# Norm broadcast and first loads in the head of a fused attention and channel-mix kernel

## The chip, the cores and the metric

One core of one Trainium2 chip runs the kernel. The metric is the device time of one execution in microseconds (us); smaller is better. The engines are named as in the profile: PE is TensorE's matmul stream and PEld its weight loads, DVE is VectorE, ACT is ScalarE, POOL is GpSimd, SP is SyncE, which here only issues DMAs.

## The reference

Two layers one after the other, in float32, for B = 4 batches of N = 6208 rows and C = 256 channels. First cross-covariance attention: the attention matrix is over channels (256 x 256), and the norms run over the rows.

```python
def _attn_ref(q, k, v, tau):
    qn = q / (np.linalg.norm(q, axis=1, keepdims=True) + 1e-06)
    kn = k / (np.linalg.norm(k, axis=1, keepdims=True) + 1e-06)
    s = kn.transpose(0, 2, 1) @ qn / tau
    s = s - s.max(-1, keepdims=True)
    a = np.exp(s)
    a /= a.sum(-1, keepdims=True) + 1e-09
    return (v @ a).astype(np.float32)
```

Then a channel mix with a shift by one row, with x the result of the first:

```python
    xk = mu_k * x + (1.0 - mu_k) * x_prev
    xr = mu_r * x + (1.0 - mu_r) * x_prev
    k = np.maximum(xk @ w_k, 0.0)
    v = k * k @ w_v
    r = 1.0 / (1.0 + np.exp(-(xr @ w_r)))
    return (r * v).astype(np.float32)
```

## The kernel before

**Tiles.** The rows of a batch are cut into NB = 12 groups of 512 and one of 64 (number 12). The second layer works on blocks of 512 rows: 48 full ones and one made of the four batches' left-over rows.

**The head.** Attention needs the whole q and k of a batch before x of that batch can be made. For batch 0 this is the head of the kernel. SP loads the rows as float32 (`head_load`, L98, eight buffers). For each piece VectorE casts to bf16 (L130 for q, L143 for k), ScalarE squares (L132, L145), and TensorE adds up norms as matmuls against a column of ones (L115) and, for k, the 256 x 256 product with q (L148, into `s_ps0`). The order is q 0 to 7, q 12, then k 0, q 8, k 1, q 9, k 2, q 10, k 3, q 11, then k 12, k 4 to k 9, and k 10 and k 11 in smaller pieces. The norms of one piece are issued after the products of the next (`flush`). Between pieces stand fillers (L194), matmuls of 512 columns into a PSUM tile that nobody reads; they keep TensorE occupied. Three of them follow k 12.

**q's norms.** All of q is in after q 11. After k 5, `root` copies the sums out of PSUM (L159) and GpSimd takes the root (L161). After k 7, `inverse` (L166, L168) adds 1e-6 and takes the reciprocal, `spread` (L176 to L179) splits the two columns into three bf16 parts, and `broadcast` (L186) makes six matmuls that spread them over all partitions into a PSUM tile of the "v" tag. After k 9 VectorE copies that tile to SBUF (`rq_bc0`, L571), where the softmax reads it (L591).

**The first loads.** GpSimd issues every load that casts from float32 to bf16, all in one queue. After k 7's cast a one-column copy (`gate`, L573) holds the queue back; then it issues v of block 0, w_k (128 x 2 x 1024 in one DMA), v of blocks 1 and 2 (L234), and q and k of the first group of batch 1 (`more_rows(1)`, L432: the group of 64 rows, which the loop's first unit reads). Behind k's root follow more groups (`more_rows`), w_r (L603), w_v (L604) and v 3. In this program a GpSimd DMA waits until the one eight before it has landed.

**From the head to the loop.** v of block 0 is transposed by TensorE (L254) and copied by ScalarE (L258); twelve fillers follow; then the softmax (L204 to L209) makes `a_sb`, and `x_first` (L275) makes the first x. It also transposes v of block 1. `wf` (L612, L613) is w_k's first 256 columns with mu folded in, for the first two up projections (L334).

**The loop.** A loop over i from -2 to 48 and j from 0 to 7 is the order of everything else, written out by hand. Step (i, j) issues the up projection of block i+1 (L339, evacuated and rectified by ScalarE at L343, squared by VectorE at L350), the gate matmul (L360) and down projection (L399, the first reader of w_v) of block i, x of block i+2 (L265, L267), the mixes (L307, L318), and units of the next batch's q and k products (L443, L447) by due times. v of blocks 2 and 3 is transposed by TensorE at j = 7 of i = -1 and i = 0; later blocks by a DMA. The first unit of batch 1 is due in step (-1, 6).

Of the kernel before, what the change touches and what calls it, by code (L numbers as in the profile page):

```python
# [14 lines left out]
OP = mybir.AluOpType  # L15
# [3 lines left out]
def kernel(  # L19
# [13 lines left out]
    nc = tc.nc  # L33
    B, N, C = q.shape
    D = C
    DF = moe_w_k.shape[1]
    P = 128
    M = 512
    S = M // P
    assert C == 256 and DF == 1024  # L40
    NB = N // M
# [47 lines left out]
    LEAD = 8  # L89
# [48 lines left out]
    def k_piece(g, s0, s1, last=False):  # L138
        rows, n = rows_of(g)
        n = s1 - s0  # L140
        f = head_load(k, 0, g, s0, s1)
        kt = pq.tile([P, S, C], BF16, name="kb", tag="kb", bufs=6)
        nc.vector.tensor_copy(kt[:rows, :n], f[:rows, :n])  # L143
        sq = pq.tile([P, S, C], BF16, name="hsq", tag="hsq", bufs=5)
        nc.scalar.activation(sq[:rows, :n], f[:rows, :n], AF.Square)  # L145
        for s in range(n):
            for ih in range(2):
                nc.tensor.matmul(s_ps0[:, ih, :], kt[:rows, s, ih * P:(ih + 1) * P], qb[g][:rows, s0 + s, :],  # L148
                                 start=first("s"), stop=last and s == n - 1, skip_group_check=True)
        flush()  # L150
        pend.append((nk_ps, "k", sq, rows, n, last))
        return kt
# [11 lines left out]
    def inverse(r, n):  # L164

        nc.vector.tensor_scalar_add(r[:, :n], r[:, :n], 1e-6)  # L166
        o = pn.tile([P, 4], F32, name="nrm_o")
        nc.vector.reciprocal(o[:, :n], r[:, :n])  # L168
        return o

    def spread(r):
        w = pn.tile([P, 3, 2], BF16, name="rw", bufs=1)
        d = pn.tile([P, 2], F32, name="rd", bufs=1)
        nc.vector.tensor_copy(w[:, 0], r[:, :2])  # L176
        nc.vector.tensor_tensor(d, r[:, :2], w[:, 0], op=OP.subtract)
        nc.vector.tensor_copy(w[:, 1], d)
        nc.vector.tensor_tensor(w[:, 2], d, w[:, 1], op=OP.subtract)  # L179
        return w  # L180

    def broadcast(w, tag, **kw):
        bc_ps = ps.tile([P, 2, P], F32, name="bc_ps", tag=tag, **kw)
        for h in range(2):
            for u in range(3):
                nc.tensor.matmul(bc_ps[:, h], w[:, u, h:h + 1].to_broadcast([P, P]), ident,  # L186
                                 start=h == 0 and u == 0, stop=u == 2, skip_group_check=True)
        return bc_ps.rearrange("p h d -> p (h d)")

    def filler(n, src=0):  # L190

        f_ps = ps.tile([P, M], F32, name="f_ps", tag="v", bufs=2)
        for u in range(n):
            nc.tensor.matmul(f_ps, ident, qb[src].rearrange("p s c -> p (s c)")[:, :M], start=u == 0, stop=u == n - 1)  # L194
# [36 lines left out]
    def v_load(i):  # L231
        b, t = blocks[i]
        v_bf = pq.tile([P, S, C], BF16, name="v_bf", tag="b2", bufs=NB + 1)
        nc.gpsimd.dma_start(v_bf, v[b, t * M:(t + 1) * M, :].rearrange("(s p) c -> p s c", p=P))  # L234
        st[i, "v"] = v_bf
# [12 lines left out]
    def v_transpose_pe(i, v_bf, s0, s1, evac):  # L248
        vT = st[i, "vT"] if (i, "vT") in st else new_vT(i)
        n = s1 - s0  # L250
        vT_ps = ps.tile([P, S, 2, P], BF16, name="vT_ps", tag="kT", bufs=3)
        for s in range(n):
            for h in range(2):
                nc.tensor.transpose(vT_ps[:, s, h], v_bf[:, s0 + s, h * P:(h + 1) * P], ident)  # L254
        if evac == "v":
            nc.vector.tensor_copy(vT[:, s0:s1], vT_ps[:, :n])
        else:
            nc.scalar.copy(vT[:, s0:s1], vT_ps[:, :n])  # L258
# [289 lines left out]
    def more_rows(n):  # L548
        while pos["load"] < min(len(loads), n):
            group_load(*loads[pos["load"]])  # L550
            pos["load"] += 1
# [6 lines left out]
    for what, g in order:  # L558
        if what == "q":
            q_piece(g, last=g == NB - 1)  # L560
        else:
            kt = k_piece(g, 0, rows_of(g)[1])
            if g < NB - LEAD or g == NB:
                filler(2 if g < NB else 3)

            if g == 5:
                nq = root(nq_ps, 2)
            if g == 7:
                bc_ps = broadcast(spread(inverse(nq, 2)), "v", bufs=2)
            if g == 9:  # L570
                nc.vector.tensor_copy(rq_bc0, bc_ps)  # L571
            if g == 7:
                nc.gpsimd.tensor_copy(gate, kt[:, 0, 0:1])  # L573
                v_load(0)
                nc.gpsimd.dma_start(w_k_sb, moe_w_k.rearrange("(ko ki) f -> ki ko f", ki=P))
                v_load(1)
                v_load(2)
                more_rows(1)
    k_piece(NB - 2, 0, 2)
    k_piece(NB - 2, 2, 4)  # L580
    k_piece(NB - 1, 0, 2)
    k_piece(NB - 1, 2, 3)
    k_piece(NB - 1, 3, 4, last=True)
    nc.sync.dma_start(mu_k_t, moe_mu_k.rearrange("(h p) -> p h", p=P))
    nc.sync.dma_start(mu_r_t, moe_mu_r.rearrange("(h p) -> p h", p=P))
    flush()
# [43 lines left out]
    for i in range(-2, NBLK):  # L630
        for j in range(8):
            T = i * 8 + j
            if i == LAST and j == 0:

                st[LAST, "res"] = pq.tile([P, S, D], F32, name="res", tag="f4", bufs=NF)
                for s in range(4):
                    gate_mm(LAST, s)
                for u in range(2):
                    gate_act(LAST, u)
            if j in (2, 6) and i != LAST:  # L640
                gate_act(i, j // 4)
            if 0 <= i + 1 < NBLK:
                up(i + 1, j)
            if j == 0 and i >= 0:
                square(i, 7)
            if j > 0 and j != 6 and 0 <= i + 1 < NBLK:
                square(i + 1, j - 1)
            if j == 5:
                finish(i, 0)
            if j == 1:  # L650
                finish(i - 1, 1)
            if i >= 0:
                if j in (0, 1, 4, 5) and i < LAST:
                    gate_mm(i, j // 4 * 2 + j % 4)
                down(i, j)
            n = i + 2
            if n == 0 and j == 0:
                x_first()
            if 0 < n < NBLK and n != LEFT:
                if j == 0:  # L660
                    x_half(n, 0)
                if j == 2:
                    x_half(n, 1)
            if n < NBLK:

                d = 4 if n != 1 else 3
                if j == d:
                    mix_delta(n)
                if j in (d + 1, d + 2):
                    mix(n, "xk", j - d - 1)  # L670
            if j == 6 and 0 <= i + 1 < NBLK:
                square(i + 1, j - 1)
            if j in (0, 1) and 0 <= i + 1 < NBLK:
                mix(i + 1, "xr", j)
            if j == 7 and 2 <= i + 3 < NPE:
                v_transpose_pe(i + 3, st.pop((i + 3, "v")), 0, S, "s")
            if j == 1 and NPE <= i + 5 < NBLK and i + 5 != LEFT:
                v_transpose_dma(i + 5)
            if j == 2 and NPE < i + 7 < NBLK and i + 7 != LEFT:
                v_load(i + 7)  # L680
            bank_x = i >= 0 and i % NB == 6 and j == 4
            if chain and (chain[0] is None or chain[0].__name__ != "bcast" or j in (4, 6)):
                f = chain.pop(0)
                if f is not None:
                    f()
                    bank_x = f.__name__ == "bcast"
            if j in (4, 6) and not bank_x or j in (3, 5) and len(norms) > 1:
                take_norm()

            near = sums and (sums[0][0] == 1 or sums[0][1] in GORD[-3:])  # L690
            if j in (2, 3, 6, 7) and near or j in (3,7) or len(sums) > (2 if near else 4):
                take_sum()
            for u in due.get(T, []):
                b, g, s = units[u]
                at = (b - 1) * (NB + 1) + GORD.index(g)
                more_rows(at + 4)
                unit(b, g, s)
                if g == GORD[-1] and s == S - 1:
                    evac_s(b)
            if i >= 0 and i // NB < B:  # L700
                bl = i // NB
                if i % NB == 2 and j == 1:
                    lst["v"] = left_load(bl)
                if i % NB == 4 and j == 3:
                    lst["t"] = left_transpose(lst["v"])
                if i % NB == 6 and j == 4:
                    left_x(bl, lst["t"])
# [35 lines left out]
```

## Time and profile before

| What | us |
|---|---|
| median of 4 runs | 507.71 (507.52 to 507.99) |
| the profiled execution | 508.19 |
| its span, first to last instruction | 506.3 |
| TensorE busy in 0 to 26 us | 17.77 |
| TensorE busy in 31 to 35 us | 3.84 of 4.00 |
| TensorE busy in 38.5 to 43 us | 4.12 of 4.50 |
| TensorE busy in 43 to 50 us | 6.76 of 7.00 |
| TensorE busy in 50 to 55 us | 4.73 of 5.00 |
| TensorE busy in 70 to 100 us | 29.79 of 30.00 |

The profile is of one execution, whose time is not the median; times of instructions are counted from the start of its span. A line of the timeline gives start, length, engine, line of the code, operation, output and inputs, shapes and how many; in brackets stands how long the engine was idle before it, and what it waited for. In a line of the chain of waits stand start, length, and who worked. A DMA's time to landing is counted from the start of its issue.

### The profile page before, as it was taken

The page shows a single profiled execution, that of the slowest core. Times are in us where ns is not written, and L with a number is a line of the kernel's source. Part 1 is how long each engine was busy: PE and PEld are TensorE (multiplying, and loading weights), DVE is VectorE, ACT ScalarE, POOL GpSimd, SP SyncE. Part 2 cuts the span into 40 slices and gives each one's busy share as a digit, 9 for nine tenths or more (in the row PEclk, how much of TensorE's full clock was granted, in tenths as well). Part 3 has the DMA queues.
Part 4 walks back from the last instruction along what each step waited for, and adds up shares of the span by engine and source line. Part 5 has one row for each costly group of instructions (what it writes and reads, how often), then busy time and mean ns, then how long its engine had stood idle before and what let it go on. Part 6 is the DMA issues. An engine that isn't in the chain of part 4 may idle for free.

```text
span 506.3 us, 9691 instructions
## 1 busy us (share of the span) xinstructions
PE 490.3 (97%) x3644; PEld 338.7 (67%) x3707; DVE 447.4 (88%) x706; ACT 430.2 (85%) x809; POOL 105.0 (21%) x145
## 2 busy tenths in 40 slices
PE   5799999999999999999999999999999999999997
PEld 2474677777676666666667666666666666666675
DVE  3468898999999999999999999999998787887875
ACT  6788999999998998998999899898787777777774
POOL 0047423332521321221441132100121000000000
PEclk9999999999999999999999999999999999999999
DMA  8999999999999999799699999963299753334123
GB/s 332 393 319 196 181 202 207 205 203 199 178 167 204 213 174 161 120 168 165 123 174 214 179 175 164 146 135 77 62 154 164 141 109 104 87 87 82 41 84 105
DMA packets 143535, 83.48 MB, mean 165 GB/s; under 512 B 51264, under 2 KB 140032, under 8 KB 143488
## 3 DMA queue, kind: packets, MB, share of 16 engines
q0 software_dynamic: 65808, 33.01, 53.1%
q1 hardware_dynamic: 77536, 49.79, 43.0%
q8 instruction: 29, 0.48, 0.4%
q14 instruction: 18, 0.15, 0.1%
q10 hardware_dynamic: 144, 0.07, 0.0%
HBM read 78.71 MB, written 25.43 MB: 206 GB/s over the span
## 4 chain that ended last, share of the span: by engine, by line
PE 83%; DVE 6%; DMA 6%; ACT 2%; issue 2%; POOL 0%; ACTq 0%; DVEq 0%
PE v_ps L399 31%; PE kT_ps L339 28%; PE g_ps L360 9%; PE xT_ps L265 7%; PE s_ps L443 6%; DMA f<-in_k_dram 3%; DMA v_bf<-in_v_dram 2%; DVE kk L350 1%; DVE acc L481 1%; DVE xk L318 1%; PE f_ps L194 1%; DVE res L412 1%; ACT kr L343 1%; DVE xr L318 1%; DMA f<-in_q_dram 1%
## 5 line engine op out<-in xcount | busy, mean ns | idle before, releaser
L343 ACT ACTIVATE kr<-kT_ps 128x512 bf16<-128x512 f32 (+1 forms) x392 | 232.3, 597 | 36.0 <-PE kT_ps L339 27.1
L399 PE MATMUL v_ps<-w_v_sb,kk 128*128 128x256 bf16 x1520 | 228.1, 273 | 0.8
L339 PE MATMUL kT_ps<-xk,w_k_sb 128*128 128x512 bf16 (+1 forms) x721 | 217.5, 377 | 1.2 <-DVE xk L318 0.3
L399 PEld LDWEIGHTS <-kk 128*128 128x128 bf16 x1520 | 148.3, 98 | 57.3
L350 DVE TENSOR_TENSOR kk<-kr 128x1024 bf16<-128x1024 bf16 (+1 forms) x196 | 133.0, 681 | 30.4 <-ACT kr L343 30.0
L447 ACT ACTIVATE sq<-qk 128x512 f32<-128x512 bf16 (+1 forms) x147 | 93.4, 635 | 0.0
L339 PEld LDWEIGHTS <-w_k_sb 128*128 128x128 bf16 x780 | 75.0, 98 | 22.4 <-issue 0.9
L360 PE MATMUL g_ps<-w_r_sb,xr 128*128 128x256 bf16 x388 | 73.6, 273 | 1.4
L267 ACT CAST X<-xT_ps 128x512 bf16<-128x512 f32 x94 | 55.5, 591 | 18.9 <-PE xT_ps L265 18.3
L318 DVE SCALAR_TENSOR_TENSOR xr<-delta,mu_r_t,X 128x512 bf16<-128x512 bf16 x96 | 71.4, 746 | 0.0
L360 PEld LDWEIGHTS <-xr 128*128 128x128 bf16 x388 | 37.9, 98 | 45.2 <-issue 1.3
L318 DVE SCALAR_TENSOR_TENSOR xk<-delta,mu_k_t,X 128x512 bf16<-128x512 bf16 x96 | 67.6, 746 | 0.0
L412 DVE SCALAR_TENSOR_TENSOR res<-res,v_ps 128x512 f32<-128x512 f32 x95 | 64.7, 681 | 0.0
L432 POOL DMA_DIRECT2D qk<-in_q_dram x39 | 28.8, 738 | 158.1 <-ACT sq L447 134.1
L405 ACT ACTIVATE res<-g_ps 128x512 f32<-128x512 f32 x97 | 57.9, 598 | 0.0
L265 PE MATMUL xT_ps<-vT,a_sb 128*128 128x512 bf16 x188 | 55.9, 379 | 0.5 <-ACT vT L258 0.5
L443 PE MATMUL s_ps<-qk 128*128 128x256 bf16 (+1 forms) x294 | 56.1, 273 | 0.0
L481 DVE TENSOR_TENSOR acc<-acc,sq 128x1024 f32<-128x1024 f32 x44 | 53.7, 1220 | 0.1
L234 POOL DMA_DIRECT2D v_bf<-in_v_dram x48 | 36.9, 771 | 61.1 <-DMA vT<-v_bf 40.8
L443 PEld LDWEIGHTS <-qk 128*128 128x128 bf16 (+1 forms) x294 | 27.7, 97 | 12.5 <-issue 1.3
L307 DVE TENSOR_TENSOR delta<-X 128x1024 bf16<-128x1024 bf16 x48 | 32.9, 686 | 0.3 <-ACT X L267 0.2
L432 POOL DMA_DIRECT2D qk<-in_k_dram x39 | 28.9, 740 | 6.6 <-DMA qk<-in_q_dram 2.1
(76 smaller groups left out, 233.9 us busy)
## 6 DMA issues: line engine op xcount, KB each, us to landing
out_dram<-res SPq DMA_DIRECT2D x47, 512.0 KB, 4.5
v_bf<-in_v_dram POOLq DMA_DIRECT2D x48, 256.0 KB, 9.1
qk<-in_q_dram POOLq DMA_DIRECT2D x36, 256.0 KB, 9.5
qk<-in_k_dram POOLq DMA_DIRECT2D x36, 256.0 KB, 10.8
f<-in_q_dram SPq DMA_DIRECT2D x12, 512.0 KB, 8.0
f<-in_k_dram SPq DMA_DIRECT2D x10, 512.0 KB, 8.8
f<-in_k_dram SPq DMA_DIRECT2D x3, 256.0 KB, 7.3
vT<-v_bf SPq DMA_TRANSPOSE x44, 8.2
```

Source lines behind the costliest of these rows:

```text
L265: nc.tensor.matmul(xT_ps, a_sb[:, b, ih, dh * P:(dh + 1) * P], vT[:, :, ih, :], start=ih == 0, stop=ih == 1)
L318: nc.vector.scalar_tensor_tensor(o[:, dh], st[i, "d"][:, dh], mu[:, dh:dh + 1], X[:, dh, c:c + M], op0=OP.mult, op1=OP.add)
L339: nc.tensor.matmul(kT_ps[:, :m], w_k_sb[:, dh, fh * P:(fh + 1) * P], xk[:, dh, :m], start=dh == 0, stop=dh == 1)
L343: nc.scalar.activation(st[i, "kr", fh // 2][:, fh % 2, :m], kT_ps[:, :m], AF.Relu, scale=RH)
L350: nc.vector.tensor_tensor(st[i, "kk"][:, fh - 1:fh + 1, :m], kr[:, :, :m], kr[:, :, :m], op=OP.mult)
L360: nc.tensor.matmul(g_ps[:, s % 2], xr[:, dh, s * P:(s + 1) * P], w_r_sb[:, dh, :], start=s % 2 == 0 and dh == 0, stop=dh == 1, skip_group_ ...
L399: nc.tensor.matmul(v_ps[:, s % 2], kk[:, fh, s * P:(s + 1) * P], w_v_sb[:, fh, :], start=s % 2 == 0 and fh == 0, stop=fh == 7, skip_group_ ...
L405: nc.scalar.activation(st[i, "res"][:, 2 * u:2 * u + 2], st.pop((i, "g", u)), AF.Tanh, scale=0.5)
L412: nc.vector.scalar_tensor_tensor(r, r, 1.0, st.pop((i, "v", u)), op0=OP.add, op1=OP.mult)
L443: nc.tensor.matmul(cov[b][:, ih, :], qk[:rows, s, 1, ih * P:(ih + 1) * P], qk[:rows, s, 0, :], start=g == GORD[0] and s == 0 and ih == 0, ...
L447: nc.scalar.activation(G["sq", s // 2][:rows, s % 2], qk[:rows, s], AF.Square)
L481: nc.vector.tensor_tensor(acc[b], acc[b], G["sq", w - 3], op=OP.add)
```

## The change

Six edits, all in the head and at the start of the loop:

- `spread` can run on another engine; for batch 0's q norms it runs on GpSimd. `inverse` and `spread` come after k 6 instead of after k 7, so ahead of `gate` in GpSimd's queue; `broadcast` comes after k 8 instead of after k 7.
- The copy of the broadcast to `rq_bc0` moves from after k 9 to after the last piece of k 11.
- The three fillers after k 12 go.
- w_k is loaded in two DMAs of 512 columns; the second stands behind v of block 1.
- `more_rows(1)` goes from the first loads. The same two DMAs are then issued by `more_rows(2)`, behind k's root and ahead of that call's own group.
- v of block 2 is transposed in step (-1, 6) instead of (-1, 7), ahead of that step's unit; block 3 stays in step (0, 7).

```diff
-    def spread(r):
+    def spread(r, eng=nc.vector):
         w = pn.tile([P, 3, 2], BF16, name="rw", bufs=1)
         d = pn.tile([P, 2], F32, name="rd", bufs=1)
-        nc.vector.tensor_copy(w[:, 0], r[:, :2])
-        nc.vector.tensor_tensor(d, r[:, :2], w[:, 0], op=OP.subtract)
-        nc.vector.tensor_copy(w[:, 1], d)
-        nc.vector.tensor_tensor(w[:, 2], d, w[:, 1], op=OP.subtract)
+        eng.tensor_copy(w[:, 0], r[:, :2])
+        eng.tensor_tensor(d, r[:, :2], w[:, 0], op=OP.subtract)
+        eng.tensor_copy(w[:, 1], d)
+        eng.tensor_tensor(w[:, 2], d, w[:, 1], op=OP.subtract)
         return w
...
-            if g < NB - LEAD or g == NB:
-                filler(2 if g < NB else 3)
+            if g < NB - LEAD:
+                filler(2)
 
             if g == 5:
                 nq = root(nq_ps, 2)
-            if g == 7:
-                bc_ps = broadcast(spread(inverse(nq, 2)), "v", bufs=2)
-            if g == 9:
-                nc.vector.tensor_copy(rq_bc0, bc_ps)
+            if g == 6:
+                rw = spread(inverse(nq, 2), nc.gpsimd)
+            if g == 8:
+                bc_ps = broadcast(rw, "v", bufs=2)
             if g == 7:
                 nc.gpsimd.tensor_copy(gate, kt[:, 0, 0:1])
                 v_load(0)
-                nc.gpsimd.dma_start(w_k_sb, moe_w_k.rearrange("(ko ki) f -> ki ko f", ki=P))
+                w_k = moe_w_k.rearrange("(ko ki) f -> ki ko f", ki=P)
+                nc.gpsimd.dma_start(w_k_sb[:, :, :DF // 2], w_k[:, :, :DF // 2])
                 v_load(1)
+                nc.gpsimd.dma_start(w_k_sb[:, :, DF // 2:], w_k[:, :, DF // 2:])
                 v_load(2)
-                more_rows(1)
     k_piece(NB - 2, 0, 2)
...
     k_piece(NB - 1, 3, 4, last=True)
+    nc.vector.tensor_copy(rq_bc0, bc_ps)
...
-            if j == 7 and 2 <= i + 3 < NPE:
-                v_transpose_pe(i + 3, st.pop((i + 3, "v")), 0, S, "s")
+            if (i, j) in ((-1, 6), (0, 7)):
+                n = 2 if i < 0 else 3
+                v_transpose_pe(n, st.pop((n, "v")), 0, S, "s" if n == 2 else "s")
```

## The prediction

> **What bounds the kernel now.** I read the page's busy table first, then the chain of waits for 20 to 60 us, then the timeline of that stretch engine by engine, then the DMA queues in windows.
>
> ```profile
> PE 490.3 (97%) x3644; PEld 338.7 (67%) x3707; DVE 447.4 (88%) x706; ACT 430.2 (85%) x809; POOL 105.0 (21%) x145
> ```
>
> TensorE is busy in 97% of the span, so past the head there is nearly nothing to win by removing a wait. The 16 us without PE work lie mostly in the first 26 us (17.77 busy of 26.00, the windows view), which no edit touches. What is left is 28 to 53 us. The chain there, in order of time (start, length, what):
>
> ```profile
> 31.08 0.69 DVE kb L143
> 31.78 0.09 DVE nrm_r L166
> 31.87 0.16 POOL gate L573
> 32.09 0.91 POOL v_bf L234
> 33.00 0.90 POOL w_k_sb L575
> 33.90 8.85 DMA v_bf<-in_v_dram
> 42.80 0.64 PE vT_ps L254 x8
> 43.46 1.02 ACT vT L258
> 44.52 0.59 PE xT_ps L265 x2
> ```
>
> The end hangs on the second v block: gate, v 0, w_k, v 1 in one GpSimd queue, landing at 42.75, then transpose, eviction, x. In the timeline, two stretches of TensorE and VectorE:
>
> ```profile
> 28.19 0.81 PE L194 MATMUL f_ps<-qb,ident 128*128 128x512 bf16 x3
> ...
> 31.08 0.69 DVE L143 CAST kb<-f 128x1024 bf16<-128x1024 f32 x1 [0.59 <-DMA f<-in_k_dram]
> ...
> 32.49 0.48 DVE L178 CAST rw<-rd 128x2 bf16<-128x2 f32 x1
> ...
> 33.08 1.32 DVE L143 CAST kb<-f 128x1024 bf16<-128x1024 f32 x2
> ...
> 33.82 1.05 PE L148 MATMUL s_ps<-qb,kb 128*128 128x256 bf16 x8 [0.16 <-DVE kb L143]
> ```
>
> The reader is to see that k8's cast starts at 33.08 although ScalarE squares the same tile at 32.37, waiting only for its DMA: six small VectorE operations from 31.69 to 33.16 stand ahead of the cast, and TensorE waits for it at 33.82.
>
> ```profile
> 38.77 2.75 PE L194 MATMUL f_ps<-qb,ident 128*128 128x512 bf16 x11
> 41.37 1.10 PE L275 MATMUL x_ps<-vT,a_sb 128*128 128x512 bf16 x4
> 42.80 0.62 PE L254 MATMUL vT_ps<-ident,v_bf 128*128 128x128 bf16 x8 [0.33 <-DMA v_bf<-in_v_dram]
> ...
> 50.73 0.49 PE L399 MATMUL v_ps<-w_v_sb,kk 128*128 128x256 bf16 x3
> 51.44 0.59 PE L265 MATMUL xT_ps<-vT,a_sb 128*128 128x512 bf16 x2 [0.22 <-ACT vT L258]
> ```
>
> Three places where the end of the head is set: fillers up to x_ps, v 1's landing, and block 2's vT. Last the GpSimd queue (q0) in 34 to 37.5 us and the same in 41 to 50 us:
>
> ```profile
> q0 software_dynamic: 576, 0.36, 93.9%
> q1 hardware_dynamic: 645, 0.11, 21.8%
> ```
>
> ```profile
> q0 software_dynamic: 3511, 1.74, 144.3%
> ```
>
> From 41 on it moves 1.74 MB in 9 us (0.193 MB/us) without a gap; in its first 3.5 us only 0.36 MB, half that rate, beside the last k rows and the two mu loads. No q0 packet lies in 33 to 34, so the first comes some 2 us after v 0's issue at 32.09.
>
> **What the Trainium skill says.** SBUF — State Buffer, Who interferes with whom: a cast in a 2-port mode and GpSimd lock each other out for a whole instruction. The trace agrees: the pow on GpSimd takes 1.12 us beside k6's cast (29.79 to 30.48), 0.72 the other time, and the 128x2 cast at 32.49 takes 0.48 instead of 0.17 beside a GpSimd DMA issue. GPSIMD Engine Reference, Instruction dispatch: consecutive Pool instructions that depend on each other need a semaphore wait between them; the four moved ones form such a chain. The trace has one such pair, at the very start (a memset at 0.74, its reader at 1.02): 0.28 us from start to start. DMA: Bandwidth & Descriptors, Anatomy of one DMA: about 2.0 us fixed for a GpSimd DMA; the 2 us to the first packet fit.
>
> **The change part by part.**
>
> *Fillers after k12 gone.* Three matmuls at 0.217 us, 0.65 us of PE from 28.19. Then k4 could start at 28.18 instead of 28.83, but the casts come with the DMA: k5's ends at 29.25, k6's at 30.48, k7's at 31.77. Each piece costs PE 1.07 us (start to start), so PE catches up with its data by k6, and this edit alone is worth nothing at k7 or later; it only exposes the casts.
>
> *Spread to GpSimd, inverse one piece earlier.* The pow ends at 30.53; VectorE's two inverse operations run at 30.57 to 30.95 in the 0.6 us idle before k7's cast: free. k8's cast then starts with its data, at about 32.37 (ScalarE's square of it) instead of 33.08: 0.71 earlier, and k8's matmuls at 33.10 instead of 33.82. The broadcast's six matmuls (0.33 us, 33.17 to 33.50), which lay in that wait, now lie behind k8. Net at the end of the k loop: 0.72 - 0.33 = 0.4 earlier, 37.9 instead of 38.3. k9's cast, from 33.66 to 34.35, is in time for PE at 34.48.
>
> *Copy of the broadcast behind the last cast.* 0.40 us on VectorE, between the last cast (ends by 36.6) and nrm_a, which waits for PE until about 38.1: covered by 1 us. The cost if that cover went is 0.4.
>
> *The price of the spread on GpSimd.* Four operations in front of the gate, v 0 and all later loads. Not shown in the trace. Below: 0.24 each (gate to the next issue, 31.85 to 32.09), 31.0 to 32.0, delay d = 0.1 or 0.2, as the gate waits for k7's cast until 31.85 anyway. Above: 0.72 each (the pow) plus one lock of 0.69: done at 34.6, d = 2.9. I take 0.3 each, the dependent pair's 0.28 rounded up, and one lock behind k7's cast: spread done by 32.7, gate 32.9, v 0 issued at about 33.1, d = 1.0. It also can hold up the casts of k7 or k8 by one small operation, 0.2, kept for the range.
>
> *What d does to the stream.* If the slow first 3.5 us are due to the k rows and mu, which go on their own, a later start loses little: 1 us of start holds some 0.1 MB of packets at the observed rate, 0.5 us at 0.193 MB/us. If it is a ramp of its own, all of d is lost; if mu alone made it slow, the stream ends even earlier. I take e = 0.4 (bounds -0.4 and d). Then v 0 lands at 37.5 + 0.4 to 0.5 = 38.0, where PE arrives at 37.9: hidden. x_ps then starts at 41.0 instead of 41.37, still behind its twelve fillers (2.6 us); VectorE's second a_sb, 41.81 before, moves 0.4 with the k loop.
>
> *w_k in halves.* Half of 0.512 MB leaves v 1's way: 0.256/0.193 = 1.3 us. v 1 lands at 42.75 - 1.3 + 0.4 = 41.85; PE asks for it at about 42.0. The 0.33 us wait goes. The folded weights read columns below 256, in the first half; the second half is needed at 46 (fh of 4 and up) and lands by 43.5. One more issue, some 0.8 us of GpSimd, is hidden while the stream is backlogged.
>
> *From x_ps to block 1.* X's second half ends at 42.8 instead of 43.19, ScalarE's vT of block 1 at 43.5 instead of 44.47, so PE's wait at 44.52 (0.23) goes. Next late is xk: 45.45 - 0.4 = 45.05; PE's third up then at 45.1 instead of 45.81. ScalarE, without a gap from 46.01 on, starts that run 0.6 earlier.
>
> *qk of group one behind the softmax.* Its two issues (0.70 + 0.59) move to 39.0, ahead of qk, w_r, w_v. It landed at 43.84 and 44.02 (issue plus time to landing); first use 48.65. Queued behind v 2 it still lands near 44.5: hidden. w_v's issue goes from 41.66 to about 42.5, but its bytes wait behind the backlog until 47, so only e moves it: it landed at 41.66 + 8.3 = 50.0, then 50.4.
>
> *v 2 a step sooner.* Same eight transposes and 1.03 us of ScalarE, ahead of kr instead of behind; it landed at 43.6 and is needed at 48.4. It takes the 0.22 us wait at 51.44 away; kk's last square has 0.5 us left to the matmul at 52.74.
>
> *Sum.* PE comes to its first w_v matmul 0.6 early, at 50.1, waits for w_v until 50.4 (0.35 left), and gets the 0.22 at x back: 0.6 us. After that everything shifts together. The profiled execution took 508.19 (span 506.3 plus 1.9 around it), so 507.6; its median is 0.48 lower, so 507.1.
>
> **The rivals.** The forecast (0.40): 507.1.
> *No collision (0.30).* Starting after the k rows, the stream loses nothing (e about -0.4), w_v at 49.6, no stall: 0.6 + 0.22, and up to 0.3 more where ScalarE's run stays ahead: 506.6. For it: half rate only in 34 to 37.5. Against: the order of bytes is nearly unchanged.
> *The stream takes all of d (0.18).* v 0 at 38.5, fillers push x_ps to 41.5; w_v at 51.0 against 50.73: +0.3 - 0.22 and a little for v 0: 507.9, no change. For it: a stream that never idles from 41 to 50 cannot make a loss good.
> *Slower (0.12).* GpSimd's small operations cost what the pow costs, d = 2.9, and the stream takes all: v 0 at 40.4, twelve fillers behind it, x_ps 2.1 late, w_v at 52.9: 509.7. It decides from d about 2, where w_v at 52.0 is over 1.0 late after the 0.22.
>
> **How the numbers follow.** 0.2%, about what a measurement of this kernel can tell from no change, is 1.0 us. A fifth of the forecast's 0.40 and three quarters of the 0.30 lie over 1.0 faster: 0.31. Slower: 0.12, and a sixth of the 0.18: 0.15. The rest, 0.54, is no change. Range 506.2 to 508.4, which leaves out the slow rival and thin tails.
>
> **What would show it.** Right: k8's cast at its DMA's landing, GpSimd's gate near 32.9, v 1 landing before PE asks, no wait at the second x of block 2. Wrong: a gate after 34 us, PE idle at v 0's transposes or ahead of the first w_v matmul for more than 0.5 us, or the gain lost again past 60 us.

## The result: slower by 0.13%

The changed kernel takes 508.39 us in the median (507.62 to 509.32) against 507.76 for the kernel before (507.12 to 508.66) on the same chips. The ratio is 1.0013, with a 95% interval of 1.0008 to 1.0017: about 0.66 us slower, where 507.1 was forecast. That is clear of noise and has the other sign than the forecast; 508.39 lies just inside the upper edge of the stated range (508.4).

The profiled execution took 509.27 us, 0.9 above the median and the second longest of 34, so its waits may be larger than typical ones. Its k rows also come about 0.5 us later than in the profile before (k 5's cast at 29.07 instead of 28.56). Steps are compared from there.

From the changed kernel's page, the busy times and the group of the down projection (line, engine, operation, tiles, shapes, count, then busy us, mean ns, and the idle time before it with what ended it):

```profile
PE 490.8 (97%) x3641; PEld 338.9 (67%) x3704; DVE 447.1 (88%) x702; ACT 430.5 (85%) x809; POOL 106.3 (21%) x150
...
L399 PE MATMUL v_ps<-w_v_sb,kk 128*128 128x256 bf16 x1520 | 228.1, 273 | 1.9 <-DMA w_v_sb<-in_moe_w_v_dram 1.1
```

But for the three fillers TensorE does the same work, in a span that is 1.1 us longer, and the down projection, for which the page of the kernel before lists no wait for a DMA, now has 1.1 us of it. The chain of waits says where that comes from (start, length, what):

```profile
38.73 0.17 DVE nrm_a L159
38.91 0.08 issue
38.99 0.71 POOL nrm_r L161
39.70 2.57 POOL qk L432 x4
42.27 0.14 POOL w_r_sb L605
42.41 0.53 issue
42.95 9.25 DMA w_v_sb<-in_moe_w_v_dram
52.20 0.04 issue
52.24 0.49 PE v_ps L399 x3
```

The chain no longer runs through v of block 1. It goes from the last k norm through k's root on GpSimd, through four qk issues (two more than before), to w_v's DMA and from there to the first down projection. TensorE's own timeline of the changed kernel (idle time in brackets):

```profile
42.89 0.61 PE L254 MATMUL vT_ps<-ident,v_bf 128*128 128x128 bf16 x8
...
50.76 0.38 PE L360 MATMUL g_ps<-w_r_sb,xr 128*128 128x256 bf16 x2
52.24 0.49 PE L399 MATMUL v_ps<-w_v_sb,kk 128*128 128x256 bf16 x3 [1.10 <-DMA w_v_sb<-in_moe_w_v_dram]
52.57 0.59 PE L265 MATMUL xT_ps<-vT,a_sb 128*128 128x512 bf16 x2
```

The waits at v 1 (0.33 us before) and at the second x (0.22 us before) are gone, as forecast. A single new one at w_v is larger than both. w_v lands at 52.2 instead of 50.0, 1.7 us later when counted from k 5's cast. The GpSimd queue (q0; packets, MB, share of the DMA engines) shows where the time goes. In 41 to 50 us it moves 1.50 MB, where the kernel before moved 1.74:

```profile
q0 software_dynamic: 2942, 1.50, 130.9%
```

### The profile page after: what moved, and what is told of

Same layout as the page of the kernel before. It is cut to its first block, busy times and chain, and to the rows that moved or that the text cites. A ratio compares the mean times of both kernels' runs of the same rounds, so it can differ in the third digit from the quotient of the medians.

```text
span 507.4 us, 9688 instructions
## 1 busy us (share of the span) xinstructions
PE 490.8 (97%) x3641; PEld 338.9 (67%) x3704; DVE 447.1 (88%) x702; ACT 430.5 (85%) x809; POOL 106.3 (21%) x150
## 4 chain that ended last, share of the span: by engine, by line
PE 86%; DVE 6%; DMA 5%; issue 2%; POOL 1%; ACT 0%; ACTq 0%
PE v_ps L399 31%; PE kT_ps L339 28%; PE g_ps L360 9%; PE xT_ps L265 7%; PE s_ps L443 6%; DMA f<-in_k_dram 2%; PE s_ps L148 2%; DMA w_v_sb<-in_moe_w_v_dram 2%; PE f_ps L194 2%; DVE kk L350 1%; DVE acc L481 1%; DVE xk L318 1%; DVE res L412 1%; DVE xr L318 1%; DMA f<-in_q_dram 1%
## 5 line engine op out<-in xcount | busy, mean ns | idle before, releaser
L234 POOL DMA_DIRECT2D v_bf<-in_v_dram x48 | 37.0, 772 | 63.9 <-DMA vT<-v_bf 41.3
```

## The experiments

The sets of experiments ran on different chips, so their times are compared by the ratios to the kernel before, which ran beside each. Traces are of one execution each. Three explanations of w_v's late landing stood at the start: A, the two small qk loads behind k's root make the large loads' issue late; B, the spread on GpSimd starts all loads late; C, w_k in halves moves more slowly.

### The small loads early again

```diff
                 v_load(2)
+                more_rows(1)
     k_piece(NB - 2, 0, 2)
```

> The changed kernel with the first group's two qk loads put back behind v of block 2, ahead of k's root. Theory A (the loads behind k's root are issued too late: two more issues, 1.1 us, stand ahead of w_v, and TensorE's 1.10 us wait for w_v is the loss): w_v lands by about 51.0 instead of 52.2, the wait falls below 0.3 us, time about 1.0 us under the changed kernel's 508.4, so 507.4 or a ratio near 0.999. Theory B (the spread on GpSimd starts the whole stream of loads 0.8 us later): no change, 508.3. Theory C (halves of w_k move more slowly than the whole): no change, 508.3.

Measured: 507.19 us, ratio 0.9988 (0.9982 to 0.9995). That is 0.25 points, or 1.27 us, under the changed kernel, and faster than the kernel before. In its chain two qk issues stand between the root and w_r, and w_v lands 1.9 us earlier than in the changed kernel, 1.3 us when counted from k 5's cast (28.46 here):

```profile
38.39 0.72 POOL nrm_r L161
39.11 1.52 POOL qk L432 x2
40.63 0.66 POOL w_r_sb L606
41.29 9.04 DMA w_v_sb<-in_moe_w_v_dram
50.33 0.04 issue
50.37 0.49 PE v_ps L399 x3
```

Its GpSimd queue moves nearly as much again in 41 to 50 us as in the kernel before:

```profile
q0 software_dynamic: 3467, 1.72, 143.1%
```

A holds. w_v is still on the chain, but TensorE waits for it by 0.2 us only.

### The spread on VectorE

```diff
-                rw = spread(inverse(nq, 2), nc.gpsimd)
+                rw = spread(inverse(nq, 2))
```

> The changed kernel with the spread's four operations on VectorE again, still after k 6. Theory B: gate and all loads 0.8 us sooner, w_v lands at 51.4, wait 0.3 us, time about 507.6. Theory A: little, 508.2, since w_v's issue hangs on k's root and not on the gate. Theory C: 508.3.

Measured: 508.75, ratio 1.0016 (1.001 to 1.0023), not told from the changed kernel's 1.0013. B is not supported. The test is not clean, though: the gate did not come sooner. k 7's cast, which it waits for, now stood behind the spread's four operations on VectorE (31.55, the last of them at 31.47), and the gate's own copy, beside k 8's cast, took 0.63 us instead of 0.19:

```profile
32.30 0.63 POOL L573 COPY gate<-kb 128x1 bf16<-128x1 bf16 x1 [1.87 <-DVE kb L143]
32.87 0.91 POOL L234 DMA_DIRECT2D v_bf<-in_v_dram  x1
```

Counted from k 5's cast (28.45 here), v 0 is issued 4.4 us later, 3.8 in the changed kernel and 3.5 in the kernel before. So the spread on GpSimd costs the stream of loads 0.3 us of start, and 0.6 more of it here changed nothing that can be measured, though the k loop has also lost its gain (9.75 us from k 5's cast to v 0's transposes, 9.49 in the changed kernel).

### w_k whole

```diff
-                nc.gpsimd.dma_start(w_k_sb[:, :, :DF // 2], w_k[:, :, :DF // 2])
+                nc.gpsimd.dma_start(w_k_sb, w_k)
                 v_load(1)
-                nc.gpsimd.dma_start(w_k_sb[:, :, DF // 2:], w_k[:, :, DF // 2:])
```

> The changed kernel with w_k loaded whole, ahead of v of block 1. Theory C: the stream regains its rate, w_v lands at 50.5 to 51, time about 507.5, less what a late v of block 1 costs (0.3). Theories A and B: v of block 1 lands 1.3 us later, at 42.4, just in time for TensorE at 42.9, w_v as late as before: 508.3 to 508.6.

Measured: 507.73, ratio 0.9997 (0.9989 to 1.0006), 0.8 us better than the changed kernel by the ratios. So C has a share too. Its profiled execution took 508.75, 1.0 above its median and the longest of its 13, and w_v lands at 51.7 in it, so this profile does not show the typical case. v of block 1 lands at 41.4, behind the whole w_k.

### Only the small loads late

```diff
                 v_load(2)
-                more_rows(1)
     k_piece(NB - 2, 0, 2)
```

> The kernel before with only the first group's qk loads moved behind k's root. Theory A: w_v lands 1 to 2 us later than 50.0, TensorE waits up to 1.3 us for it at 50.7: 508.3 to 508.9, a ratio of 1.001 to 1.0025. Theories B and C: no change, 507.7.

Measured: 507.98, ratio 1.0003 (0.9994 to 1.0011): no change, where A had 1.001 or more. The queue does slow down. In the windows view (window; busy us of PE, PEld, DVE, ACT, POOL; clock; DMA share; GB/s) of 42 to 43 us the DMA share is 1.04 with 96 GB/s, against 1.45 with 189 in the kernel before. w_v lands 0.7 us later, at 50.7, exactly when TensorE, which is not ahead in this kernel, asks for it. So this edit alone costs nothing that can be measured; it costs where the rest of the change is in place.

### The small loads second

```diff
-    more_rows(2)
+    for n in (1, 0):
+        group_load(*loads[n])
+    pos["load"] = 2
```

This is made from the changed kernel: the small pair stays behind k's root, but behind the large pair.

> The changed kernel with the first group's two qk loads behind k's root as in the change, but behind the second group's pair instead of ahead of it. If the loss is that the stream of loads runs dry because the first large load behind k's root is issued 1.1 us later, it is gone here: the DMA share in 41 to 44 us is back over 1.40, w_v lands near 50.5, time about 507.3, a ratio near 0.999. If the small loads as such upset the stream wherever they stand behind the root, it stays at 508.4 to 508.8 (1.0015).

Measured: 507.20, ratio 0.9986 (0.9979 to 0.9993). Behind the root, the order of GpSimd's issues is now large, large, small, small:

```profile
38.46 0.72 POOL L161 TENSOR_TENSOR nrm_r<-nrm_a,half 128x2 f32<-128x2 f32 x1 [2.08 <-DVE nrm_a L159]
39.14 0.78 POOL L432 DMA_DIRECT2D qk<-in_q_dram  x1
39.91 0.75 POOL L432 DMA_DIRECT2D qk<-in_k_dram  x1
40.64 0.56 POOL L432 DMA_DIRECT2D qk<-in_q_dram  x1
41.17 0.56 POOL L432 DMA_DIRECT2D qk<-in_k_dram  x1
```

w_v is issued at 42.41, as long after the root's start (3.95 us) as in the changed kernel (3.96), and still the loss is gone: the queue moves 1.73 MB in 41 to 50 us. So what matters is not when w_v is issued, but when the first large load behind the root is. The times show it better than this profile does: its execution took 507.95, the second longest of 18, w_v landed at 50.89 where 50.5 was expected, and TensorE waited 0.76 us for it.

```profile
q0 software_dynamic: 3419, 1.73, 142.6%
```

### A pause in place of the loads

```diff
+    for _ in range(3):
+        nc.gpsimd.memset(dly, 0.0)
     more_rows(2)
```

This is made from the kernel with the small loads early; `dly` is a scratch tile of 128 x 512.

> The first group's qk loads early again (as in x1_qk_early), and three plain fills of a scratch tile on GpSimd between k's root and the next loads, about 1.1 to 1.4 us in which nothing is issued. If the late issue alone is the cause: DMA share in 41 to 44 us falls to 1.3, w_v lands near 52, time 508.3 to 508.6 as in the changed kernel. If the small loads' place is the cause: at most the 0.3 us by which w_v's margin is short, 507.2 to 507.6.

Measured: 508.03, ratio 1.0003 (0.9995 to 1.0011), some 0.75 us above the kernel without the pause. The fills took 1.68 us, and the queue moves as little in 41 to 50 us as in the changed kernel:

```profile
q0 software_dynamic: 2958, 1.47, 132.3%
```

A pause alone slows the queue and costs 0.75 of the 1.27 us. It lasted longer than the two small issues (1.1 us) and still cost less than the 508.3 to 508.6 expected if the late issue were all. That the small loads in this place cost some more than their time of issue is possible; the next run was meant to tell.

### The small loads a second time, for nothing

```diff
+    for t in (q, k):
+        nc.gpsimd.dma_start(dmy[:L, 0 if t is q else 1], src_rows(t, 1, NB)[:, 0])
     more_rows(2)
```

> x1_qk_early with the first group's two small loads issued a second time behind k's root, into a scratch tile that nobody reads: the place and the 1.1 us of issue as in the change, but nothing waits for them. If the 1.1 us of late issue are all: as y2_wait_only (which waited 1.6 us) or less, 507.7 to 508.0. If small loads at the point where the stream is dry cost more than their time of issue: 508.3 to 508.6, as the changed kernel.

Measured: 509.19, ratio 1.0036 (1.0023 to 1.0049), worse than both, with four of its twelve executions over 510 us. It does not settle the question: with two DMAs more, GpSimd ran into the limit of eight in flight and stood idle for 0.54 us ahead of w_r's issue and for 1.13 ahead of w_v's, so that w_v went out at 43.93 and TensorE waited 1.4 us for it. What remains of the 1.27 us beside the pause stays open.

### w_k whole and the small loads early

Both edits, that of the small loads and that of w_k, are made to the changed kernel together:

```diff
                 v_load(2)
+                more_rows(1)
...
-                nc.gpsimd.dma_start(w_k_sb[:, :, :DF // 2], w_k[:, :, :DF // 2])
+                nc.gpsimd.dma_start(w_k_sb, w_k)
                 v_load(1)
-                nc.gpsimd.dma_start(w_k_sb[:, :, DF // 2:], w_k[:, :, DF // 2:])
```

> x1_qk_early with w_k loaded whole. By the prediction the halves take away a 0.33 us wait for v of block 1, so without them 507.5. If v of block 1 lands in time in most executions anyway (41.4 in x3_wk_whole, against 42.75 in the profile of before): 507.2, no difference.

Measured: 506.96, ratio 0.9983 (0.9976 to 0.9991), 0.86 us faster than the kernel before. The halves gain nothing: v of block 1 lands at 41.3 behind the whole w_k and TensorE asks at 41.8. With the small loads early they cost nothing clear of noise either (0.9983 against 0.9988); with the loads late they cost 0.8 us (0.9997 against 1.0013). They do slow the queue. The GpSimd queue of the changed kernel in 37.5 to 41 us, and of this one:

```profile
q0 software_dynamic: 813, 0.53, 113.9%
```

```profile
q0 software_dynamic: 936, 0.65, 124.7%
```

In this stretch every profile with halves moved 152 to 170 GB/s and every one with the whole w_k 192 to 201 (the windows view). w_v lands at 49.5 here, before TensorE's first use at 49.9, and at 50.3 with halves.

### w_v in halves

```diff
-    nc.gpsimd.dma_start(w_v_sb, moe_w_v.rearrange("(fo fi) d -> fi fo d", fi=P))
+    w_v = moe_w_v.rearrange("(fo fi) d -> fi fo d", fi=P)
+    nc.gpsimd.dma_start(w_v_sb[:, :4], w_v[:, :4])
+    nc.gpsimd.dma_start(w_v_sb[:, 4:], w_v[:, 4:])
```

First on the kernel with the small loads early (and w_k in halves), then also with w_k whole:

> x1_qk_early with w_v in two DMAs of four row blocks each; the first down projection reads the first alone. In x1_qk_early TensorE still waits for w_v, to 50.37, some 0.4 us. If w_v's landing is what bounds the head: its first half lands at 49.0, the wait goes, time about 506.8, ratio 0.998. If something else is late next: 507.2.

> The changed kernel with the small loads early, w_k whole and w_v in halves: the candidate for the best. If w_v still holds the head back in y3_early_whole (506.96) in some executions: 506.6 to 506.8. If it no longer bounds, 507.0.

Measured: 506.90, ratio 0.9983 (0.9975 to 0.9990), and 506.85, ratio 0.9984 (0.9977 to 0.9992). In both, TensorE has no wait at w_v. Against 507.19 the first gain is inside the intervals; against 506.96 there is none. Once w_v lands in time, halving it is worth nothing that can be measured. These two and the one before are the fastest versions, about 0.85 us under the kernel before.

### The two helpful parts alone

The step of block 2 alone, on the kernel before, is the last hunk of the change.

> The kernel before with block 2 transposed a step sooner and nothing else. If the prediction's term holds, the 0.22 us wait at the second x goes: 507.5 against 507.75, ratio 0.9995. If ScalarE, which has no gap there, only trades one wait for another: no change.

Measured: 507.38, ratio 0.9992 (0.9984 to 1.0000). The wait at the second x is gone from TensorE's timeline:

```profile
50.17 0.49 PE L399 MATMUL v_ps<-w_v_sb,kk 128*128 128x256 bf16 x3
50.49 0.59 PE L265 MATMUL xT_ps<-vT,a_sb 128*128 128x512 bf16 x2
```

The norm part alone is the change without the edits to the loads and to block 2.

> The kernel before with the norm part alone: spread on GpSimd after k 6, broadcast after k 8, copy behind the last cast, no fillers after k 12; loads and block 2 as before. The profiles show the k loop 0.26 us shorter: 507.5, ratio 0.9995. If it is this part that makes y3_early_whole faster than before by 0.85 us: 507.0, ratio 0.9985. If the gain of y3_early_whole lies in the two parts together only, neither run moves by over 0.3.

Measured: 507.13, ratio 0.9991 (0.9983 to 0.9999). The broadcast now lies between k 8 and k 9 (TensorE's timeline):

```profile
33.25 1.05 PE L148 MATMUL s_ps<-qb,kb 128*128 128x256 bf16 x8
34.34 0.49 PE L186 MATMUL bc_ps<-ident,rw 128*128 128x128 bf16 x6
34.82 1.05 PE L148 MATMUL s_ps<-qb,kb 128*128 128x256 bf16 x8
```

That is about 0.4 and 0.46 us by the ratios; the first interval touches no change, the second is just clear of it. Their sum, 0.86, is what the kernel with both gains, but each interval is wide enough (0 to 0.8 us) that the agreement proves little. The traces are sharper: from the second x of block 1 to that of block 2 it is 5.20 us with the old step (the kernel before, only the small loads late, the norm part alone) and 4.97 or 4.98 with the new one where TensorE has no wait at w_v (the step alone, w_k whole with the small loads early), and from k 5's cast to v 0's transposes 9.77 us without the norm part and 9.49 with it.

## Why the prediction was wrong

With the norm part and the new step of block 2 in place, the four ways to load stand like this (median us, ratio to before):

| | w_k whole | w_k in halves |
|---|---|---|
| small loads early | 506.96, 0.9983 | 507.19, 0.9988 |
| small loads late | 507.73, 0.9997 | 508.39, 1.0013 (the change) |

The 0.86 us that two parts gain are given back by two others, 1.5 us in all by the ratios (0.9983 to 1.0013).

**The step that failed** is "qk of group one behind the softmax", and in it the sentence that w_v's "bytes wait behind the backlog until 47, so only e moves it". It took the backlog of the kernel before as given and priced the 1.1 us of later issue at nothing. The runs show its price: 1.27 us for the small loads ahead of the large ones, nothing that can be measured for the same loads behind them, 0.75 us for a pause alone. Counted from k 5's cast, w_v lands after 23.1 us in the changed kernel, 21.9 with the small loads early and 21.5 in the kernel before. The pause and the exchanged order show that it is the first large load behind the root that counts.

How full the queue still was can be worked out from q0's own bytes. When GpSimd comes back from k's root at 39.67, v 0, w_k, v 1 and v 2 (1.31 MB) have been issued, and 0.67 MB of them have been moved. The small loads add 0.07 MB. The first large load was issued at 40.74, and with the 2 us to a first packet that I had read from v 0 it cannot start before 42.7; by then 1.26 MB are through and 0.12 MB are left. The queue is not empty by this sum, only thin. The same sum leaves 0.19 to 0.30 MB in the kernel before and in the six experiments whose queue moved 1.69 to 1.74 MB in 41 to 50 us, and 0.12 MB or less in six that moved 1.43 to 1.57 (the changed kernel, the spread on VectorE, w_k whole, only the small loads late, the pause, and the step of block 2 alone, whose loads stand as before but came faster). The run with the small loads a second time does not fit (0.22 MB left, 1.51 moved), but its later issues were held up by the limit of eight. All this is from one profile of each kernel. Why a thin queue then stays slow is open: of the 0.24 MB that the changed kernel is behind in 41 to 50 us, some 0.2 are lost after 44, when the next loads had long been issued. One of the rivals rested on a stream that never idles; whether the edits leave it without gaps was never worked out.

**A second effect of the same edit**, on VectorE, was not in the prediction. Behind the small loads the first large issue falls just ahead of the softmax's first scaling of `a_sb`. Before, and changed:

```profile
40.23 0.76 POOL L432 DMA_DIRECT2D qk<-in_k_dram  x1
...
40.75 0.36 DVE L209 TENSOR_SCALAR a_sb<-e_sb,sm 128x256 bf16<-128x256 f32 x1
```

```profile
40.74 0.78 POOL L432 DMA_DIRECT2D qk<-in_q_dram  x1
...
40.97 0.67 DVE L209 TENSOR_SCALAR a_sb<-e_sb,sm 128x256 bf16<-128x256 f32 x1
```

In the five profiles with small loads first behind the root (the changed kernel, the spread on VectorE, w_k whole, only the small loads late, the small loads a second time) this operation takes 0.66 to 0.69 us and TensorE needs 4.31 to 4.35 us from v 0's transposes to v 1's; in the other experiments it is 0.35 to 0.37 us, and 3.90 to 4.11. So TensorE comes to w_v some 0.35 us later. In the changed kernel's profile the wait for w_v hides that. Where w_v is less late it may be part of the 0.5 us that the pause does not explain; no run tests it alone.

**The place was forecast, the size was not.** w_v was seen as the next bound, with 0.35 us of stall. Counted from k 5's cast, TensorE was ready for w_v only 0.1 us sooner than before (22.07 instead of 22.17 us), not 0.6; with the small loads early it was 0.44 us sooner (21.73). In the profile of the kernel before w_v had 0.7 us to spare, and moving the small loads alone is free (1.0003); it costs where the other parts have used up what there was to spare. Without this edit the rest of the change gains 0.6 us by the ratio (0.9988), as much as was forecast for all of it. Part of that agreement is luck, since the halves, counted at 0.33 us, gained nothing, and the stall, counted at 0.35, was 0.18 in that profile.

**Point by point.** The spread: GpSimd's four operations and the gate took 1.25 us from first start to gate start (31.50 to 32.75), near my 0.3 each. The delay d was 0.3 us, not 1.0: the lock lay inside the chain and cost 0.3 us (the second operation took 0.51), and the gate and v 0's issue followed 0.13 us apart, where I had 0.2 each. The k loop: 0.28 us shorter, counted from k 5's cast to v 0's transposes (9.49 instead of 9.77 us), not 0.4; TensorE waited 0.15 us for k 9's cast. The copy of the broadcast at 37.11 was covered, as said. v 0 landed at 38.10, before TensorE at 38.56. The term for w_k's halves was wrong twice. v of block 1 did land early (41.1), but it does so with w_k whole as well: 41.3 to 41.6 in all six experiments that keep it whole. The 42.75 in the profile of before belonged to that one execution, in which all DMAs together carried 135 GB/s in 34 to 37.5 us, where these six carried 166 to 206. And the halves took rate from the stream, which the prediction did not consider. The step of block 2 was right: 0.23 us in the traces for the 0.22 forecast, 0.4 by the time (the interval holds both). The slow rival had the wrong mechanism: it looked for the loss at the gate, not behind k's root.

## What to carry to other kernels

A backlog in a load queue hides late issue only while it lasts: before an issue is moved or put ahead of others, add up what that queue still has outstanding and how long it lasts, and compare it with the first large load's issue plus its time to the first packet. Here the queue slowed down with 0.12 MB or less left at that point, about 0.6 us of its work, and kept its rate with 0.19, so leave a margin. Ask also what else runs on the engines at the new moment of the issue. When an edit brings an engine forward, look up the slack of every load that it will then meet first, since the edits share that slack. And a wait read from one profiled execution may be that execution's; a second profile of a kernel with the same stage tells.

## What was not expected of the hardware

- w_k in two loads of 512 columns instead of one of 1024 lowered what the GpSimd queue moved in 37.5 to 41 us from 192 to 201 GB/s to 152 to 170, in every profile. Why is not shown.
- After the queue had become thin, its share stayed low for 6 us (1.31 in 44 to 50 us, 1.45 in the kernel before), although later loads had been issued by then. Why is not shown either.
- The gate's copy of one column took 0.63 us beside a cast on VectorE, and the second of the four spread operations 0.51 us beside k 7's cast; alone such operations took 0.18 to 0.20. The scaling of `a_sb` that starts 0.2 us after a large qk issue took 0.67 us instead of 0.36.
